# A three-tile input load cut into two around the value weights, and six matmuls on ones behind the first transposes

## The chip, the cores and the metric

The kernel runs on one core of a Trainium2 chip. The metric is the device time of one execution in microseconds (us). The engines are named as in the profile: PE is TensorE's matmuls, PEld its weight loads, DVE VectorE, ACT ScalarE, POOL GpSimd and SP SyncE, which here only issues transfers (DMAs). SPq and PEq are the instruction sequencers of SP and PE.

## What is computed

One block on x of 2048 tokens by 512 channels, bfloat16, with 32 heads of 16 and a hidden width of 1792. Layer norm feeds a linear attention with softmax feature maps and a gated bilinear unit; both are added to x.

```python
xn = _layernorm(x, axis=-1)
q, k, v = xn @ wqkv                      # three parts of 512 columns, 32 heads of 16
pq, pk = q @ w_phi, k @ w_phi            # 16 by 16 for each head
phi_q = concat([softmax(pq), softmax(-pq)])
phi_k = concat([softmax(pk), softmax(-pk)])
kv, z = einsum("bhsf,bhsd->bhfd", phi_k, v), einsum("bhsf->bhf", phi_k)
o = (phi_q @ kv) / (phi_q . z + 1e-6)
h = (xn @ w_gate) * (xn @ w_up)
out = x + o @ wo + h @ w_down
```

## The kernel before

The tokens are 16 tiles of 128. All work is recorded first, as steps: a step belongs to one engine and holds one instruction, or on PE a group of matmuls, with what it reads and writes. From the regions that the steps touch, `_Sched` derives who waits for whom. Then `_order` (L790) writes the order of each engine's queue by list scheduling: it takes the step that can start first by its own cost figures (`cost`, `lat`, and for a transfer `at`, the time at which it is taken to land). Each engine then runs its queue strictly in that order, with semaphore waits where a step needs another engine's result. So an `at` in the source is no time of the chip, but it moves instructions in the queues.

The start of the program is what the change touches.

- SP's queue, in order: x of tile 0 (L352, 128 KB), x of tiles 1 to 3 in one transfer (L353, 384 KB), the two halves of the value weights (L354, 256 KB each: 128-row groups 0 and 1, then 2 and 3), gate and up weights for the first four of 14 column blocks (L357, 512 KB each), w_phi (L358), x of tiles 4 to 7 (L360), the key weights by a transposing transfer (L361), two more pairs of gate and up weights, and behind these the transposing transfers of the normalised tiles 4 and on, each of which waits for DVE.
- PE begins with 30 matmuls of a constant tile of ones (L367) into PSUM bank 3. They compute nothing that is used; they run while the first x is on its way.
- Tiles 0 to 3 (`RAW = 4`, loop at L727) are not normalised before they are used. For each, `emit_centred` (L416) takes the row sum (L424 on DVE, for tile 2 an ACT activation with an accumulator, L420) and makes 512 x minus the sum (L427). `emit_T` (L472) transposes the centred tile on PE by four 128x128 matmuls with an identity, in two halves of two, and ACT copies each half out of PSUM (L277). `emit_moments` (L412, L413 and L414) and `emit_root` (L433: L434 and L437 on POOL) compute the variance and its root, which come in later as a scale. `k_pe` (L552) multiplies the transposed tile by the value weights: four matmuls of 128x512, one for each 128-row group, so the first two need the first half of the value weights and the last two the second. For tiles 0 to 3 these four are separate steps, so the scheduler can put other work between them.
- Then come `make_wbd` (L391, four POOL multiplications, L393), `wprime` (L493), which folds w_phi into the key weights by 32 small matmuls, and the main loop: key softmaxes for all tiles beside the gate and up matmuls (`glu`, L585), the kv sums, the same for the queries, and the output matmuls (`final`, L684).

PE's queue before starts so: 30 matmuls on ones; tile 0's four transposes; tile 0's first value matmul; the transposes of tiles 1 and 2; four value matmuls (tile 0's other three and tile 1's first); tile 3's transposes; the other eleven value matmuls; five groups of four gate and up matmuls; `wprime`. DVE's queue: row sum and centring of tile 0, of tile 1, centring of tile 2, row sum and centring of tile 3, then L386 (a mask) and the moments of tiles 0 to 3.

All matmuls are issued from line 297 and all plain ACT copies from line 277, so groups have to be told apart by shape and time.

Of the kernel before, what the change touches and what calls it, by code (L numbers as in the profile page):

```python
# [12 lines left out]
PE, ACT, DVE, POOL, SP = "PE", "ACT", "DVE", "POOL", "SP"  # L13
# [168 lines left out]
def bass_parallel_sum__linear_kernel_hedgehog__glu_gated_bilinear__prompt_kernel(  # L182
    nc: bass.Bass,
    A_x: bass.AP,
    A_wqkv: bass.AP,
    A_w_phi: bass.AP,
    A_wo: bass.AP,
    B_x: bass.AP,
    B_w_gate: bass.AP,
    B_w_up: bass.AP,  # L190
    B_w_down: bass.AP,
    out: bass.AP,
):
    with ExitStack() as es:
        _build(nc, es, A_x, A_wqkv, A_w_phi, A_wo, B_w_gate, B_w_up, B_w_down, out)


def _build(nc, es, A_x, A_wqkv, A_w_phi, A_wo, B_w_gate, B_w_up, B_w_down, out):
# [59 lines left out]
    def sbv(name, lo, n):  # L258
        off = layout[name] + lo
        return arena[:, off:off + n]  # L260
# [5 lines left out]
    def bank(b, lo=0, n=512):  # L266
        return psum[:, b * 512 + lo: b * 512 + lo + n]

    sc = _Sched(nc)
# [16 lines left out]
    def dve(fn, reads, writes, n, rate=1.0, fixed=65.0, prio=None):  # L286
        return sc.step(DVE, fn, reads=reads, writes=writes, cost=fixed + rate * n / 0.96, lat=150.0, prio=prio)
# [4 lines left out]
    def mms(items, prio=None, cold=False):  # L292

        def fn(e):
            ins = None
            for o, l, r, a, z in items:
                ins = e.matmul(o, lhsT=l, rhs=r, start=a, stop=z)  # L297
            return ins
        reads = []
        writes = []  # L300
        c = 0.0
        for o, l, r, a, z in items:
            reads += [l, r]
            writes.append(o)
            c += max(25.0, o.free_size() / 2.4 + 2.3) * (1.92 if cold else 1.0)
        return sc.step(PE, fn, reads=reads, writes=writes, cost=c, lat=260.0, prio=prio)
# [12 lines left out]
    def x_tile(t):  # L319
        return sbv("x", t * 512, 512)  # L320
# [7 lines left out]
    wv_v = sbv("wv", 0, NQ * 512).rearrange("p (q j) -> p q j", q=NQ)  # L328
# [7 lines left out]
    def load_x(on, t0, n, at):  # L336
        return sc.dma(on, sbv("x", t0 * 512, n * 512).rearrange("p (t d) -> p t d", t=n),
                      x_flat[t0 * 128:(t0 + n) * 128, :].rearrange("(t p) d -> p t d", p=128), at=at)

    def load_w(on, dst, src, at, issue=500.0):  # L340
        return sc.dma(on, dst, src, at=at, issue=issue)
# [5 lines left out]
    def load_gu(on, f0, n, at):  # L347
        return [load_w(on, v[:, :, f0 * 128:(f0 + n) * 128],
                       src[:, f0 * 128:(f0 + n) * 128].rearrange("(q p) f -> p q f", p=128), at)
                for v, src in ((wg_v, B_w_gate), (wu_v, B_w_up))]  # L350

    load_x(SP, 0, 1, 2950.0)  # L352
    load_x(SP, 1, 3, 4200.0)  # L353
    wv_loads = [load_w(on, wv_v[:, 2 * h:2 * h + 2, :],  # L354
                       A_wqkv[h * 256:(h + 1) * 256, 1024:1536].rearrange("(q p) j -> p q j", p=128), at)
                for on, h, at in ((SP, 0, 5000.0), (SP, 1, 6000.0))]
    load_gu(SP, 0, 4, 8300.0)  # L357
    sc.dma(SP, wphi_v, bass.AP(tensor=A_w_phi.tensor, offset=A_w_phi.offset, ap=[[16, 128], [2048, NQ], [1, 16]]),  # L358
           at=10900.0)
    load_x(SP, 4, 4, 11850.0)  # L360
# [5 lines left out]
    one = nc.const_aps.tensor(1.0, [128, 128], BF16)  # L366
# [45 lines left out]
    def emit_moments(t):  # L412
        dve(lambda e: e.bn_stats(stats_v[:, t, 0:6], x_tile(t)), [x_tile(t)], [stats_v[:, t, 0:6]], 512)  # L413
        dve(lambda e: e.bn_aggr(mv_v[:, t, :], stats_v[:, t, 0:6]), [stats_v[:, t, 0:6]], [mv_v[:, t, :]], 6)  # L414

    def emit_centred(t):  # L416

        total = lnt_v[:, 1, 8 + t:9 + t]
        if t in ACT_MEAN:
            sc.step(ACT, lambda e: e.activation(out=xn_tile(t), in_=x_tile(t), func=ACTF.Copy, accum_out=total),  # L420
                    reads=[x_tile(t)], writes=[xn_tile(t), total], cost=700.0, lat=180.0)
            again = [xn_tile(t)]
        else:
            dve(lambda e: e.tensor_reduce(out=total, in_=x_tile(t), axis=AX.X, op=ALU.add), [x_tile(t)], [total], 512,  # L424
                fixed=130.0)
            again = []
        dve(lambda e: e.tensor_scalar(out=xn_tile(t), in0=x_tile(t), scalar1=float(D), scalar2=total, op0=ALU.mult,  # L427
                                      op1=ALU.subtract), again + [x_tile(t), total], [xn_tile(t)], 512, rate=0.5)
# [4 lines left out]
    def emit_root(t):  # L433
        pool(lambda e: e.tensor_scalar(out=veps(t), in0=mv_v[:, t, 1:2], scalar1=1e-5, scalar2=float(D * D),  # L434
                                       op0=ALU.add, op1=ALU.mult),
             [mv_v[:, t, :]], [veps(t)], 1)
        pool(lambda e: e.tensor_tensor(out=rstd_v[:, t, 0:1], in0=veps(t), in1=mhalf[:, 0:1], op=ALU.pow),  # L437
             [veps(t), mhalf], [rstd_v[:, t, 0:1]], 1, rate=155.0, fixed=400.0)
# [33 lines left out]
    def emit_T(t):  # L472
        for h in range(2):
            b = (5, 6, 7, 4)[(2 * t + h) % 4]
            mms([(bank(b, q * 128, 128), xn_tile(t)[:, (2 * h + q) * 128:(2 * h + q + 1) * 128], ident, True, True)
                 for q in range(2)], cold=t < 2)
            act_op(xnT_v[:, 2 * h:2 * h + 2, t * 128:(t + 1) * 128],
                   bank(b, 0, 256).rearrange("p (q s) -> p q s", q=2))
# [73 lines left out]
    def k_pe(t):  # L552
        b = next_a()
        items = group(bank(b), [(xnT(q, t * 128, 128), wv_v[:, q, :]) for q in range(NQ)])
        if t < RAW:
            for item in items:
                mms([item])
        else:
            mms(items)
        act_op(vext_all[:, t, :, 0:64], bank(b).rearrange("p (c j) -> p c j", c=8), scale=scale_of(t))  # L560
# [166 lines left out]
    for t in range(RAW):  # L727
        first = len(sc.steps)
        emit_centred(t)
        emit_T(t)  # L730
        for st in sc.steps[first:]:
            st.urgent = True
        emit_moments(t)
        emit_root(t)
        k_pe(t)
# [192 lines left out]
```

## Time and profile before

| | us |
|---|---|
| median of 3 runs (lowest to highest) | 221.11 (221.06 to 221.14) |
| the profiled execution's own time | 219.36 |
| its span, first to last instruction | 218.1 |
| PE busy in the span | 213.1 (98%) |
| DVE busy | 194.2 (89%) |
| ACT busy | 116.0 (53%) |
| POOL busy | 10.0 (5%) |
| HBM read / written | 8.67 MB / 2.10 MB |

Matmuls are pipelined, so a busy PE in the profile says only that some matmul is on its way; the spacing of their starts tells whether PE was held up. A few matmul records are missing from the trace, at a regular distance: where the spacing is just one matmul too long, it is a record that is missing. The mean granted clock stands as 1.00 in the profile's tables, for this core without an event behind it, so the clock at the start has to be read from the spacing of equal matmuls.

### The profile page before, as it was taken

The page shows a single profiled execution, that of the slowest core. Times are in us where ns is not written, and L with a number is a line of the kernel's source. Part 1 is how long each engine was busy: PE and PEld are TensorE (multiplying, and loading weights), DVE is VectorE, ACT ScalarE, POOL GpSimd, SP SyncE. Part 2 cuts the span into 40 slices and gives each one's busy share as a digit, 9 for nine tenths or more (in the row PEclk, how much of TensorE's full clock was granted, in tenths as well). Part 3 has the DMA queues.
Part 4 walks back from the last instruction along what each step waited for, and adds up shares of the span by engine and source line. Part 5 has one row for each costly group of instructions (what it writes and reads, how often), then busy time and mean ns, then how long its engine had stood idle before and what let it go on. Part 6 is the DMA issues. An engine that isn't in the chain of part 4 may idle for free.

```text
span 218.1 us, 3598 instructions
## 1 busy us (share of the span) xinstructions
PE 213.1 (98%) x1289; PEld 104.5 (48%) x1312; DVE 194.2 (89%) x551; ACT 116.0 (53%) x195; POOL 10.0 (5%) x29
## 2 busy tenths in 40 slices
PE   7999999999999999999999999999999999999996
PEld 6444444444445544444445444444544444454454
DVE  4787999999999389999998899999999999999532
ACT  4578986548353599965553687553544353121000
POOL 2451000110002000000000000000000000000000
DMA  5999440035901340000000002263466547546931
GB/s 186 321 281 298 113 157 3 0 64 155 310 3 23 75 99 0 0 0 3 0 0 2 3 0 48 52 96 74 96 120 125 109 108 108 125 109 127 141 72 50
DMA packets 47442, 19.91 MB, mean 91 GB/s; under 512 B 37440, under 2 KB 47424, under 8 KB 47424
## 3 DMA queue, kind: packets, MB, share of 16 engines
q1 hardware_dynamic: 47424, 19.69, 39.5%
q8 instruction: 10, 0.16, 0.3%
q14 instruction: 8, 0.07, 0.1%
HBM read 8.67 MB, written 2.10 MB: 49 GB/s over the span
## 4 chain that ended last, share of the span: by engine, by line
PE 77%; DVE 15%; ACT 3%; DMA 2%; issue 2%; SPq 1%; DVEq 0%
PE ps L297 77%; DVE arena L598 4%; DVE arena L542 4%; ACT arena L277 3%; DMA arena<-in_A_wqkv_dram 2%; DVE arena L522 2%; DVE arena L574 2%; DVE arena L571 1%; DVE arena L528 1%; DVE arena L450 1%; DVE arena L481 1%; SPq L165 1%; DVE arena L703 0%; DVE arena L452 0%; DVEq L887 0%
## 5 line engine op out<-in xcount | busy, mean ns | idle before, releaser
L297 PE MATMUL ps<-arena 128*128 128x512 bf16 (+5 forms) x1259 | 209.9, 327 | 2.3 <-ACT arena L277 1.0
L297 PEld LDWEIGHTS ps<-arena 128*128 128x128 bf16 (+1 forms) x1282 | 101.4, 98 | 110.8 <-ACT arena L277 1.7
L277 ACT ACTIVATE arena<-ps 128x512 bf16<-128x512 f32 (+2 forms) x140 | 72.0, 571 | 45.5 <-PE ps L297 38.5
L277 ACT ACTIVATE arena<-arena 128x1024 bf16<-128x1024 bf16 (+1 forms) x40 | 38.5, 977 | 30.0 <-DVE arena L528 29.8
L542 DVE TENSOR_TENSOR arena<-arena 128x512 f32<-128x512 bf16 (+3 forms) x128 | 48.5, 389 | 0.2
L598 DVE TENSOR_TENSOR arena<-ps,arena 128x512 bf16<-128x512 f32 x56 | 38.1, 681 | 3.5 <-PE ps L297 2.3
L522 DVE TENSOR_TENSOR arena<-arena 128x64 bf16<-128x64 bf16 (+3 forms) x128 | 31.2, 269 | 3.8 <-ACT arena L277 3.6
L528 DVE TENSOR_TENSOR arena<-arena 128x1024 bf16<-128x1024 bf16 x32 | 21.6, 677 | 0.1
L703 DVE TENSOR_TENSOR arena<-ps,arena 128x512 bf16<-128x512 f32 (+2 forms) x13 | 8.3, 641 | 7.1 <-PE ps L297 7.1
L574 DVE TENSOR_TENSOR arena<-arena 128x1024 bf16<-128x1024 bf16 x16 | 10.8, 676 | 0.0
L277 ACT ACTIVATE arena<-ps,arena 128x512 bf16<-128x512 f32 x12 | 7.9, 682 | 2.8 <-PE ps L297 1.7
L571 DVE RECIPROCAL arena<-arena 128x64 bf16<-128x64 f32 x16 | 8.7, 541 | 0.0
L675 DVE TENSOR_TENSOR arena<-ps,arena 128x512 bf16<-128x512 f32 x12 | 8.1, 676 | 0.1
L450 DVE BATCH_NORM_STATS2 arena<-arena 128x6 f32<-128x512 bf16 x12 | 8.0, 680 | 0.0
L667 DVE RECIPROCAL arena<-ps 128x32 f32<-128x32 f32 x16 | 5.5, 346 | 1.8 <-PE ps L297 1.8
L654 DVE TENSOR_TENSOR arena<-arena 128x512 bf16<-128x512 bf16 x16 | 6.6, 411 | 0.0
L651 DVE RECIPROCAL arena<-arena 128x32 f32<-128x32 f32 x16 | 5.4, 336 | 0.0
L481 DVE TENSOR_SCALAR arena<-arena 128x512 bf16<-128x512 bf16 x12 | 4.3, 399 | 0.7 <-POOL arena L458 0.7
L424 DVE TENSOR_REDUCE arena<-arena 128x1 f32<-128x512 bf16 x3 | 2.0, 683 | 3.1 <-DMA arena<-in_A_x_dram 3.1
L297 PE MATMUL ps<-const-bfloat16-1.0 128*128 128x128 bf16 x30 | 3.4, 313 | 0.8 <-PEq L913 0.8
L297 PEld LDWEIGHTS ps<-const-bfloat16-1.0 128*128 128x128 bf16 x30 | 3.1, 149 | 0.8 <-issue 0.8
L458 POOL TENSOR_TENSOR arena<-arena 128x4 f32<-128x4 f32 x3 | 3.1, 1047 | 0.3
(31 smaller groups left out, 29.7 us busy)
## 6 DMA issues: line engine op xcount, KB each, us to landing
out_dram<-arena SPq DMA_DIRECT2D x15, 128.0 KB, 2.0
arena<-in_B_w_down_dram SPq DMA_DIRECT2D x1, 1792.0 KB, 7.5
arena<-in_B_w_gate_dram SPq DMA_DIRECT2D x2, 640.0 KB, 6.8
arena<-in_B_w_up_dram SPq DMA_DIRECT2D x2, 640.0 KB, 8.0
arena<-in_A_x_dram SPq DMA_DIRECT2D x1, 1024.0 KB, 5.8
arena<-arena SPq DMA_TRANSPOSE x44, 2.6
arena<-in_A_wqkv_dram SPq DMA_DIRECT2D x2, 256.0 KB, 4.0
arena<-in_B_w_gate_dram SPq DMA_DIRECT2D x1, 512.0 KB, 5.3
```

The lines of the kernel that those rows point to most:

```text
L277: return e.activation(out=out_ap, in_=in_ap, func=func, scale=scale, **kw)
L297: ins = e.matmul(o, lhsT=l, rhs=r, start=a, stop=z)
L450: dve(lambda e, t=t: e.bn_stats(stats_v[:, t, 0:6], x_tile(t)), [x_tile(t)], [stats_v[:, t, 0:6]], 512)
L522: dve(lambda e, dst=dst, src=src, k=k: e.tensor_tensor(out=dst, in0=src[:, :, 0:k], in1=src[:, :, k:2 * k], op=ALU.max), [src], [dst], 16 ...
L528: dve(lambda e: e.tensor_tensor(out=p4, in0=p4, in1=src[:, :, None, :].to_broadcast([128, 16, 16, 4]), op=ALU.subtract), [pst, src], [pst] ...
L542: dve(lambda e, dst=dst, src=src, k=k: e.tensor_tensor(out=dst, in0=src[:, :, 0:k], in1=src[:, :, k:2 * k], op=ALU.add), [src[:, :, 0:2 * ...
L571: dve(lambda e: e.reciprocal(out=rs, in_=sm), [sm], [rs], 64, rate=6.0)
L574: dve(lambda e: e.tensor_tensor(out=e4, in0=e4, in1=r4[:, :, None, :].to_broadcast([128, 16, 16, 4]), op=ALU.mult), [ek_v[:, t, :], rs], [ ...
L598: dve(lambda e: e.tensor_tensor(out=dst, in0=bank(bu), in1=gr, op=ALU.mult), [bank(bu), gr], [dst], 512, prio=-1.0)
L654: dve(lambda e: e.tensor_tensor(out=e1, in0=e1, in1=rs[:, :, None, :].to_broadcast([128, 8, 16, 4]), op=ALU.mult), [e1, rs], [e1], 512, ra ...
L675: dve(lambda e: e.tensor_tensor(out=o4, in0=n4, in1=w4, op=ALU.mult), [nd[:, :, 0:64], w], [o], 512)
L703: dve(lambda e: e.tensor_tensor(out=og, in0=ob, in1=xs, op=ALU.add), [ob, xs], [og], c1 - c0, prio=-2.0)
```

## The change

The load of x for tiles 1 to 3 is cut in two: tiles 1 and 2 (256 KB) stay ahead of the value weights' halves, tile 3 (128 KB) goes behind them. The due times (`at`) of these and of the first gate and up weights are set anew. Behind tile 0's transposes, six more matmuls on the constant ones are put on PE, into bank 3 as the 30 at the start, made dependent on the transposes so that they stand behind them.

```diff
     load_x(SP, 0, 1, 2950.0)
-    load_x(SP, 1, 3, 4200.0)
-    wv_loads = [load_w(on, wv_v[:, 2 * h:2 * h + 2, :],
-                       A_wqkv[h * 256:(h + 1) * 256, 1024:1536].rearrange("(q p) j -> p q j", p=128), at)
-                for on, h, at in ((SP, 0, 5000.0), (SP, 1, 6000.0))]
-    load_gu(SP, 0, 4, 8300.0)
+    def load_v(h, at):
+        return load_w(SP, wv_v[:, 2 * h:2 * h + 2, :],
+                      A_wqkv[h * 256:(h + 1) * 256, 1024:1536].rearrange("(q p) j -> p q j", p=128), at)
+
+    load_x(SP, 1, 2, 3850.0)
+    load_v(0, 5050.0)
+    load_v(1, 6200.0)
+    load_x(SP, 3, 1, 6500.0)
+    load_gu(SP, 0, 4, 8600.0)
...
         emit_T(t)
         for st in sc.steps[first:]:
             st.urgent = True
+        if t == 0:
+            mms([(bank(3, 0, 128), one, one, True, True)] * 6, cold=True).deps.append(sc.by_eng[PE][-2])
         emit_moments(t)
```

What the scheduler makes of it: on PE the six matmuls on ones stand between tile 0's transposes and its first value matmul, and tile 3's transposes move behind nine value matmuls where they stood behind five. On DVE, L386 and tile 0's moments instruction (L413) move ahead of tile 3's row sum, and tile 1's aggregation (L414) moves behind tile 2's L413. SP has one transfer more, the fifth of its queue. Behind that, PE's queue holds the same instructions in the same order.

## The prediction

> **What bounds the kernel now.** I read the page first, then the chain of waits, then the timeline of the first 16 us, then what PE waited for and the windows of the span.
>
> ```profile
> PE 213.1 (98%) x1289; PEld 104.5 (48%) x1312; DVE 194.2 (89%) x551; ACT 116.0 (53%) x195; POOL 10.0 (5%) x29
> PE 77%; DVE 15%; ACT 3%; DMA 2%; issue 2%; SPq 1%; DVEq 0%
> ```
>
> PE ends the run, but its busy time hides stalls, so I go to the chain (start, length, what):
>
> ```profile
> 2.23 4.33 DMA arena<-in_A_wqkv_dram
> 6.57 0.05 issue
> 6.61 1.04 PE ps L297 x7
> 7.71 6.65 PE ps L297 x30
> ...
> 95.82 10.74 PE ps L297 x49
> 106.56 0.05 issue
> 106.61 10.74 PE ps L297 x49
> ```
>
> 49 records start 10.79 us (106.61 - 95.82) before the next group. With one missing record that is 50 matmuls of 0.216 each: 512 columns with no gap. So from 6.6 on PE runs dense, and before it the chain is one transfer: the second half of the value weights (issued 2.23, landed 6.57). Now the first 16 us:
>
> ```profile
> 0.83 3.36 PE L297 MATMUL ps<-const-bfloat16-1.0 128*128 128x128 bf16 x30 [0.83 <-PEq L913]
> 2.94 0.69 DVE L424 TENSOR_REDUCE arena<-arena 128x1 f32<-128x512 bf16 x1 [2.94 <-DMA arena<-in_A_x_dram]
> ...
> 4.07 0.61 PE L297 MATMUL ps<-arena 128*128 128x128 bf16 x4
> 4.21 0.63 ACT L420 ACTIVATE arena<-arena 128x512 bf16<-128x512 bf16 x1 [2.15 <-DMA arena<-in_A_x_dram]
> 4.21 0.69 DVE L424 TENSOR_REDUCE arena<-arena 128x1 f32<-128x512 bf16 x1 [0.20 <-DMA arena<-in_A_x_dram]
> ...
> 5.52 9.40 PE L297 MATMUL ps<-arena 128*128 128x512 bf16 x79 [0.84 <-ACT arena L277]
> ...
> 6.18 0.35 DVE L427 TENSOR_SCALAR arena<-arena 128x512 bf16<-128x512 bf16 x1
> ...
> 6.61 7.24 PEld L297 LDWEIGHTS ps<-arena 128*128 128x128 bf16 x38 [0.39 <-DMA arena<-in_A_wqkv_dram]
> ...
> 11.69 1.83 POOL L393 TENSOR_TENSOR arena<-arena 128x128 bf16<-128x128 bf16 x4
> ```
>
> PE alone between 6.4 and 6.8 us:
>
> ```profile
> 6.18 0.83 PE L297 MATMUL ps<-arena 128*128 128x512 bf16 x2
> ```
>
> There are two stalls. Tile 0's last transpose starts at 4.36 (4.07 + 0.61, less a length of 0.31); PE issues nothing more until 5.52. The row names ACT, but ACT had made the first copy by 5.2 (L277, from 4.84, 0.38 for one), and the first half of the value weights landed at 5.38 (issued 1.71, 3.7 to landing): that is what released PE. The second stall is the weight load at 6.61, 0.05 after the second half landed. The last views tell how far a gain at the start reaches:
>
> ```profile
> PE ps L297 <- ACT arena L277: 1.0, 2, 0.8
> PEld ps L297 <- DMA arena<-in_A_wqkv_dram: 0.4, 1, 0.4
> ```
>
> ```profile
> 15.08:23.20 8.12, 8.12 (x38) 3.72 (x38) 6.36 (x21) 7.09 (x14) 1.27 (x2) 1.00 1.21 280
> 23.20:58.30 35.10, 34.89 (x161) 15.87 (x163) 35.08 (x92) 23.60 (x39) 1.37 (x2) 1.00 0.38 110
> 58.30:218.10 159.80, 156.97 (x980) 76.74 (x996) 143.00 (x416) 76.54 (x126) 1.26 (x2) 1.00 0.32 62
> ```
>
> These waits are nearly all that PE has (columns of the windows: length, then busy PE, PEld, DVE, ACT, POOL, clock, DMA share, GB/s). PE's work after 6.6 is the same in both kernels, so whatever it starts earlier there it should end earlier.
>
> **The transfers.** x of tile 0 lands at 2.9 (0.79 + 2.1) in both. The three-tile load lands at 4.2 (1.25 + 2.9), 0.43 per tile. The weight halves follow at 5.38 and 6.57, 1.19 each. So tiles 1 and 2 land near 2.9 + 2 x 0.43 = 3.77, and the halves one tile earlier, by 0.43: at 4.95 and **6.14**. Bounds for the second half: tile 3's bytes cost 0.59 at the halves' own rate (5.98), or 0.35 at the best rate shown, 376 GB/s between 6 and 7 us (6.22). Tile 3's x now closes the same megabyte that the second half closed: **6.57**. Bounds: 6.45, if the new order spares the slow stretch between 4 and 5 us (242 GB/s against 336 before it) some 0.1; above, if it finishes in step with the next 128 KB of the gate load, which takes (8.06 - 6.57)/4 = 0.37: 6.94.
>
> **PE, step by step.** The ones of the start come every 0.105 ((3.36 - 0.31)/29, 0.31 being one matmul's own length). Six cost 0.64 at that pace, from 4.47 to 5.11, and lie wholly in the first stall. The first value matmul needs the first half (4.95 + 0.10, the distance seen before: 5.05) and ACT's copy. ACT's copy stood behind L420, which with its accumulator held ACT from 4.21 to 4.84; now L420 starts at 3.8, and the copy waits only for tile 0's transposes: 4.50 + 0.36 = 4.86. So the ones decide: 5.11, **0.40 earlier** than 5.52. Were the clock full by then, six would take 0.33 and 5.05 would decide; the cost of the ones is 0 to 0.06, and I take 0.06 (a gain of their own is the clock rival, below). The transposes of tiles 1 and 2 take (6.18 - 5.52 - 0.216)/8 = 0.055 each, 5.52 being tile 0's first value matmul and 6.18 its second; with two value matmuls PE is at 5.99. DVE is in time: tile 1 centred by 4.01 + 0.69 + 0.35 = 5.05, tile 2 by 5.35, needed at 5.33 and 5.55.
>
> Next late is the second half: 6.14 + 0.05 = 6.19 against 6.61, 0.42 earlier. Seven more value matmuls at 0.216 bring PE to 7.70, at tile 3's transposes. Next late is their input: landing 6.57, L424 0.69, L427 0.35 and 0.11 of hand-overs: **7.72**. DVE would have waited for x from 5.99 on; L386 and one L413 fill the time before that. From there PE has 4 x 0.055 + 27 x 0.216 = 6.05 to `wprime`: 13.77. Before, tile 3's transposes started three matmuls after 6.61, at 7.27, and the count runs 7.27 + 0.22 + 31 x 0.216 = 14.19. **Gain 0.42.** The two gates are about level, so either being late shows in full and either being early gains nothing: I take 0.40.
>
> **What must be ready 0.4 earlier.** POOL: tile 3's sum and centring now hold DVE at 6.59 to 7.66, and tile 1's aggregation ends near 9.08 (8.73 before). POOL's second root then ends 0.09 later, and the four L393, which follow without a break, end at 13.61 for 13.52. PE needs them at 13.77: 0.16 of cover; beyond it, every 0.1 costs 0.1. The added issue takes SP 0.47 to 0.51 (rows of its neighbours), and everything behind it on SP is issued that much later. In full, that means: gate 8.06 to 8.6, needed 9.45; up 9.75 to 10.25, needed 10.32; w_phi 9.9 to 10.4, needed 11.7; x of tiles 4 to 7 11.3 to 11.8, needed 12.4; key weights 13.16 to 13.66, needed 13.77. All are covered, up and key weights by 0.1 only. I take no delay: these transfers land 5 to 8 us after their issue, so they queue for bytes, and the bytes are the same. The later gate and up loads land over 1 us before use, and the transposing transfers wait on DVE.
>
> **The sum.** 218.1 - 0.40 = 217.7 of span; 219.36 - 0.40 = 218.96 for that execution. The median stands 1.75 above the profiled execution; I carry the difference over: 221.11 - 0.40 = **220.7**. What a measurement of this kernel can tell from no change is 0.2%, 0.44 us, so the forecast stands just inside it.
>
> **Rivals.** *Tile 3 late* (the other side). The end moves by (landing of tile 3's x) - 6.99, since landing + 1.15 + 6.05 is to be held against 14.19. In step with the gate load's first quarter (6.94) the gain is 0.05. At 6.99 it is gone, at 7.43 the run is 0.2% slower, and landing together with the whole gate load (8.06) costs 1.07: 222.2. For it: five loads are under way at once, and a load has landed only with its last piece. Against it: before, loads landed in the order of their issue, at steps that fit their bytes.
>
> [...]
>
> *Given back to DVE.* From 23.2 to 58.3 DVE is busy 35.08 of 35.10 us and the chain runs through it. If its sequence does not move, PE arrives early and waits: gain 0 to 0.2, 220.9 to 221.1. Against: ahead of it DVE has 1.76 idle in 8.12 us, waiting for what PE and ACT make, and behind it idles 16.8 of 159.8; so it should move along.
>
> *The clock.* The ones may do more than fill. Equal matmuls come every 0.105 until 4.4 and every 0.055 at 5.8, so the clock doubled in or just after the stall. If timed executions, which take 1.75 longer than the profiled one, stay at half pace longer because PE falls idle at 4.5, the ones keep it busy and win some of that: up to 1.75, 219.4. Against: the profiled execution was at full pace in spite of the idle time, and three timed runs agree within 0.08. [...]
>
> **How the numbers follow.** Forecast (gain 0.2 to 0.65) 0.62; tile 3 late 0.16; given back 0.13; clock 0.09. Faster by over 0.2%: 0.47 of the forecast's share (both gates a little early) and the clock case, 0.38. Slower by over 0.2%: two thirds of tile 3 late, and a little for the thin covers, 0.12. The rest, 0.50, lies within. The range takes in the early bounds with part of the clock case (220.1) and tile 3 landing at 7.4 (221.5).
>
> **What would show it.** Right: first value matmul at 5.1, the second half's wait ended near 6.2, tile 3's transposes at 7.7, `wprime` near 13.9, the last PE group ending 0.4 earlier. Wrong: a DMA wait above 0.3 before tile 3's L424 beyond 6.6; PE waits on POOL or a transfer before `wprime`; new PE waits on DVE between 17 and 58; matmuls still 0.105 apart after 5.2.

## The result

| | before | after |
|---|---|---|
| median of 22 runs (lowest to highest), us | 221.09 (219.19 to 223.09) | 219.74 (219.10 to 220.20) |
| runs above 220.7 | 14 of 22 | 0 of 22 |
| the profiled execution's own time | 219.36 | 219.10 |
| its span | 218.1 | 217.8 |

The ratio after to before is 0.9959, with a 95% interval of 0.9940 to 0.9977: faster by 0.2 to 0.6%, or 0.9 us (0.0041 x 221.09). The medians differ by more, 1.35, since the median of before lies in the upper of two groups of runs. The forecast was 220.7, a gain of 0.40. The median of 219.74 lies below the range's lower end of 220.1; by the ratio it would be 220.2 (221.11 x 0.9959), just inside. The profiled pair differs by 0.26 only.

The runs of before fall into two groups with a gap between 220.18 and 220.96: eight around 219.8 and fourteen around 221.2. The three runs shown at the start (221.06 to 221.14) all came from the upper group, and the profiled execution from the lower one. These 22 runs of the changed kernel have no upper group.

### The profile page after: what moved, and what is told of

It is laid out like the page before. It is cut to its first block, busy times and chain, and to the rows that moved or that the text cites. A ratio compares the mean times of both kernels' runs of the same rounds, so it can differ in the third digit from the quotient of the medians.

```text
span 217.8 us, 3610 instructions
## 1 busy us (share of the span) xinstructions
PE 213.0 (98%) x1295; PEld 104.5 (48%) x1318; DVE 194.2 (89%) x551; ACT 116.0 (53%) x195; POOL 10.0 (5%) x29
## 4 chain that ended last, share of the span: by engine, by line
PE 77%; DVE 15%; ACT 3%; issue 2%; DMA 2%; SPq 1%; DVEq 0%
PE ps L297 77%; DVE arena L602 4%; DVE arena L546 4%; ACT arena L277 3%; DMA arena<-in_A_wqkv_dram 2%; DVE arena L526 2%; DVE arena L578 2%; DVE arena L575 1%; DVE arena L532 1%; DVE arena L454 1%; DVE arena L485 1%; SPq L165 1%; DVE arena L707 0%; DVE arena L456 0%; DVEq L893 0%
## 5 line engine op out<-in xcount | busy, mean ns | idle before, releaser
L428 DVE TENSOR_REDUCE arena<-arena 128x1 f32<-128x512 bf16 x3 | 2.1, 684 | 3.5 <-DMA arena<-in_A_x_dram 3.5
```

## The profile after

The page of the changed kernel, its busy time, its chain and its groups:

```profile
PE 213.0 (98%) x1295; PEld 104.5 (48%) x1318; DVE 194.2 (89%) x551; ACT 116.0 (53%) x195; POOL 10.0 (5%) x29
...
PE 77%; DVE 15%; ACT 3%; issue 2%; DMA 2%; SPq 1%; DVEq 0%
...
L297 PE MATMUL ps<-const-bfloat16-1.0 128*128 128x128 bf16 x36 | 3.6, 282 | 0.8 <-PEq L919 0.8
```

The ones are x36 for x30; apart from them no engine's busy time moved by more than 0.1 us (PE 213.1, ACT 116.0 before). The timeline of the changed kernel's first 16 us (start, length, engine; lines from L354 on now stand four lower in the source, so L424 of before is L428, L393 is L397):

```profile
0.83 3.09 PE L297 MATMUL ps<-const-bfloat16-1.0 128*128 128x128 bf16 x30 [0.83 <-PEq L919]
...
4.14 0.40 PE L297 MATMUL ps<-arena 128*128 128x128 bf16 x4 [0.23 <-DVE arena L431]
...
4.38 0.51 PE L297 MATMUL ps<-const-bfloat16-1.0 128*128 128x128 bf16 x6
...
4.90 0.88 PE L297 MATMUL ps<-arena 128*128 128x512 bf16 x9
...
6.33 8.31 PE L297 MATMUL ps<-arena 128*128 128x512 bf16 x70 [0.55 <-DMA arena<-in_A_wqkv_dram]
6.66 0.69 DVE L428 TENSOR_REDUCE arena<-arena 128x1 f32<-128x512 bf16 x1 [0.54 <-DMA arena<-in_A_x_dram]
...
7.79 0.60 PEld L297 LDWEIGHTS ps<-arena 128*128 128x128 bf16 x7 [0.27 <-DVE arena L431]
...
10.42 3.15 PEld L297 LDWEIGHTS ps<-arena 128*128 128x128 bf16 x16 [0.30 <-DMA arena<-in_B_w_up_dram]
...
11.84 1.83 POOL L397 TENSOR_TENSOR arena<-arena 128x128 bf16<-128x128 bf16 x4
...
13.99 1.98 PEld L297 LDWEIGHTS ps<-arena 64*128 64x128 bf16 x40 [0.42 <-DMA arena<-in_A_wqkv_dram]
```

The long gap from 4.68 to 5.52 is closed: tile 0's transposes, six ones, first value matmul at 4.90. The wait for the second half of the value weights is still there and ends at 6.33 (6.61 before). Tile 3's transposes start behind a DVE wait near 7.8, and `wprime` (the 64-row weight loads) at 13.99, 14.28 before. At 10.42 there is a wait that before did not have: for the up weights. In all 14 traces of this study, 201.78 or 201.79 us lie between `wprime`'s first weight load and the start of PE's last matmul. So the differences between these kernels, and between two executions of one, arise ahead of `wprime`, in the first 14 to 17 us; only e12's end is 0.6 us later on top of that (2.45 us behind PE's last matmul, 1.84 or 1.85 elsewhere).

The weight load of `wprime` in the kernel before:

```profile
14.28 1.77 PEld L297 LDWEIGHTS ps<-arena 64*128 64x128 bf16 x39 [0.42 <-issue]
```

## The experiments

Theory A, the forecast: the new order of the loads brings the second half and all behind it forward; the ones only fill. Theory B, the clock: with PE idle behind tile 0's transposes, part of the executions stay at half pace for longer, and the ones prevent it.

One table of the traces first, in us; the text below refers to it. "Full pace" is between the start of the last matmul that is spaced as at half pace (0.107 for 128 columns, 0.427 for 512) and the first at full pace (0.055, 0.216). "Idle" is PE's idle time between tile 0's transposes, with the ones where they stand behind them, and the next work of the tiles, by the brackets of PE's rows (where another place is named, the idle time there). The four landings are the completions of the loads. "On record" is the time from which the trace records full granted clock; eight of the traces hold such a record, and the views of the profile do not print it.

| trace | full pace | on record | idle | second half | gate | up | key weights | `wprime` |
|---|---|---|---|---|---|---|---|---|
| before | 4.36 to 5.52 | - | 0.84 | 6.57 | 8.06 | 9.75 | 13.16 | 14.28 |
| e3 before again | 8.68 to 9.08 | 8.93 | 0.68 | 6.66 | 8.35 | 10.15 | 13.51 | 15.64 |
| e2 ones only | 3.66 to 3.85 | 3.82 | 0.46 | 6.63 | 8.30 | 10.01 | 13.41 | 14.34 |
| e9 ones only | 4.87 to 5.39 | - | 0.18 | 6.86 | 8.31 | 10.02 | 13.40 | 14.57 |
| e8 halves due later | 6.00 to 6.22 | - | 0.22 | 6.59 | 8.20 | 10.01 | 13.38 | 14.46 |
| after | 3.34 to 3.52 | 3.46 | under 0.2 | 6.29 | 8.69 | 10.38 | 13.71 | 13.99 |
| e4 after again | 4.81 to 5.00 | 4.95 | 0.19 | 6.87 | 8.68 | 10.35 | 13.66 | 14.58 |
| e10 after again | 6.29 to 6.67 | - | none | 6.15 | 8.18 | 10.30 | 13.62 | 14.32 |
| e1 loads only | 5.64 to 5.84 | - | 0.54 | 6.85 | 9.89 | 11.40 | 14.70 | 15.00 |
| e5 twelve at the start | 6.37 to 7.04 | - | 1.78, ahead of the transposes | 6.48 | 9.75 | 11.25 | 14.56 | 14.85 |
| e6 twelve behind | 5.03 to 5.21 | 5.15 | none | 6.51 | 10.08 | 11.55 | 14.85 | 15.16 |
| e7 x all ahead | 4.30 to 4.51 | 4.49 | 1.85 | 7.37 | 9.61 | 11.05 | 14.39 | 15.34 |
| e11 one value load | 3.87 to 4.12 | 4.09 | 0.32 | 5.89 | 7.76 | 9.45 | 12.88 | 14.04 |
| e12 three loads | 9.58 to 10.32 | 10.19 | 0.93, ahead of the transposes | 6.46 | 8.28 | 9.98 | 13.32 | 16.67 |

**The loads alone.** The changed kernel without the six ones behind tile 0.

```diff
-        if t == 0:
-            mms([(bank(3, 0, 128), one, one, True, True)] * 6, cold=True).deps.append(sc.by_eng[PE][-2])
```

> The new load order without the six matmuls on ones. Transfer theory (the earlier value weights make the whole gain of 1.35 us in the median): median as the changed kernel, 219.7 +- 0.3, with its narrow spread of about 1 us. Clock theory (some executions stay at half pace for some 3.4 us more when PE idles behind tile 0's transposes, which costs up to 1.7 us; the ones prevent it, and the loads alone are worth about 0.3): median 220.3 to 220.9, spread over 2 us, since the idle time is still about 0.5 us long.

219.90 (219.06 to 221.57, 12 runs), before 220.40 beside it, ratio 0.9976 [0.9946, 1.0007]; 2 of 12 runs above 220.7, against 14 of 29 of before. The median fits theory A (219.7 +- 0.3) and misses what theory B expected (220.3 to 220.9); the interval of the ratio holds 1, so the run decides little by itself. PE's weight loads in its trace:

```profile
5.12 0.14 PEld L297 LDWEIGHTS ps<-arena 128*128 128x128 bf16 x2 [0.77 <-ACT arena L277]
...
8.35 0.61 PEld L297 LDWEIGHTS ps<-arena 128*128 128x128 bf16 x7 [0.26 <-DVE arena L431]
...
11.44 3.13 PEld L297 LDWEIGHTS ps<-arena 128*128 128x128 bf16 x16 [0.75 <-DMA arena<-in_B_w_up_dram]
15.00 0.90 PEld L297 LDWEIGHTS ps<-arena 64*128 64x128 bf16 x35 [0.42 <-DMA arena<-in_A_wqkv_dram]
```

The wait for the up weights, 0.30 in the changed kernel's profile, is 0.75 here. From the weight load of tile 3's transposes to `wprime` PE takes 6.20 when nothing else is late (13.99 - 7.79; the second trace of the changed kernel has 14.58 - 8.37 = 6.21). Here it takes 6.65, so the late up weights cost 0.45.

**The ones alone.** The kernel before with the same two lines put in, its loads untouched.

> The old load order with the six matmuls on ones. Transfer theory: as the kernel before, 221.1 +- 0.2 in the median, spread over 2 us. Clock theory: median 219.9 to 220.3 and a spread of about 1 us, as of the changed kernel, but some 0.3 later because the second half of the value weights still lands near 6.6.

219.91 (219.02 to 220.60, 12 runs), ratio 0.9968 [0.9940, 0.9996]; none above 220.7. Theory B expected 219.9 to 220.3, theory A 221.1. So the ones alone take the upper group away. Either part alone ends at the same median here: the parts do not seem to add, though for the loads alone the gain is not clear of noise.

**Before again**, unchanged (no edit), as a run of its own.

> The kernel before once more, for a second trace of it and more times. Clock theory: times in two groups, near 219.8 and near 221.3; if this trace is one of the slow group, its matmuls are 0.107 us (128 columns) and 0.427 us (512 columns) apart for up to 3.4 us after 5.5. Transfer theory: every trace has full pace from 5.5 on, and a slow execution shows later landings instead.

220.52 (219.16 to 223.37, 12 runs), ratio 0.9987 [0.9949, 1.0024]; 5 of 12 above 220.7. This profile caught an execution above the split (220.74). PE's first value matmul and then its weight loads in it:

```profile
5.39 10.89 PE L297 MATMUL ps<-arena 128*128 128x512 bf16 x79 [0.68 <-ACT arena L277]
```

```profile
5.39 0.19 PEld L297 LDWEIGHTS ps<-arena 128*128 128x128 bf16 x2 [0.94 <-ACT arena L277]
...
7.08 0.15 PEld L297 LDWEIGHTS ps<-arena 128*128 128x128 bf16 x1 [0.28 <-issue]
7.50 0.15 PEld L297 LDWEIGHTS ps<-arena 128*128 128x128 bf16 x1 [0.28 <-ACT arena L277]
7.93 0.15 PEld L297 LDWEIGHTS ps<-arena 128*128 128x128 bf16 x1 [0.28 <-issue]
8.36 6.86 PEld L297 LDWEIGHTS ps<-arena 128*128 128x128 bf16 x34 [0.28 <-issue]
15.64 0.43 PEld L297 LDWEIGHTS ps<-arena 64*128 64x128 bf16 x26 [0.42 <-issue]
```

One weight load goes with each value matmul. From 7.08 to 8.36 they come every 0.42 or 0.43, half the pace of 0.216; the profile names a wait (ACT) for one of them only, and its step is no longer than the others. In the first trace of this kernel `wprime` came at 14.28; here it comes 1.36 later, and the span is 219.5 for 218.1. The delay of this execution is PE's clock, which the trace records as full only from 8.93 on.

**After again**, the changed kernel without an edit.

> The changed kernel once more, for a second trace and more times. [...]

219.93 (219.11 to 221.70, 12 runs), before 221.11, ratio 0.9964 [0.9937, 0.9990]; one run above 220.7, at 221.70, so with the six ones too an execution can come out that late. It was not profiled.

**Fewer ones at the start**, with the changed kernel: PE idles ahead of tile 0's transposes in place of behind them.

```diff
-    mms([(bank(3, 0, 128), one, one, True, True)] * 30, cold=True)
+    mms([(bank(3, 0, 128), one, one, True, True)] * 12, cold=True)
```

> The changed kernel with 12 instead of 30 matmuls on ones at the start, so that PE idles from about 2.1 to 4.1 us. [...] Transfer theory: the ones hide behind the first load anyway, 219.7 +- 0.2.

220.47 (219.58 to 221.10, 12 runs), ratio 0.9988 [0.9962, 1.0015]; 4 of 12 above 220.7. Nothing that is used was taken away and the first x lands as before, yet the median is 0.54 above the changed kernel's beside it, and 4 of 12 runs are above 220.7 for 1 of 12. Resampling the runs gives -0.1 to 1.1 for the difference of medians, so an idle PE seems to cost time even where nothing waits for PE, but this run alone does not show it. The profiled execution was one of the faster ones (219.94); its clock doubled between 6.37 and 7.04.

**Twelve ones behind tile 0** in place of six, with the planner's cost for them halved so that the order stays.

```diff
-            mms([(bank(3, 0, 128), one, one, True, True)] * 6, cold=True).deps.append(sc.by_eng[PE][-2])
+            filler = mms([(bank(3, 0, 128), one, one, True, True)] * 12, cold=True)
+            filler.deps.append(sc.by_eng[PE][-2])
+            filler.cost /= 2
```

> The changed kernel with 12 instead of 6 ones behind tile 0's transposes, all else in the same order. Clock theory: nothing left to win, since six already close the gap; in executions whose doubling is early the 12 end near 5.05 and cost nothing, in late ones they end near 5.7 and cost up to 0.6: median 219.8 to 220.1, highest up to 220.9. If more activity brings the doubling forward (a count of matmuls decides): 219.4 or less.

219.91 (219.26 to 220.46, 12 runs), ratio 0.9964 [0.9937, 0.9992]; none above 220.7. With the idle time filled, six more ones brought nothing here (219.93 with six, in the run of the changed kernel above).

**x of tile 3 in a load of its own, but ahead of the halves**, with the six ones.

```diff
-    load_x(SP, 1, 3, 4200.0)
+    load_x(SP, 1, 2, 4200.0)
+    load_x(SP, 3, 1, 4200.0)
```

> The old order of bytes (x of tiles 1 and 2, x of tile 3, then the two halves) with the six ones, so that only the extra transfer is new beside the run with ones alone. If transfers only queue for bytes: gate, up and key weights land as in the old order (8.1 to 8.4, 9.8 to 10.2, 13.2 to 13.5), times as with ones alone, 219.9 +- 0.2. If the extra issue delays all that is behind it on SP: they land 0.4 to 0.6 later (8.7, 10.4, 13.9), as in the trace of the changed kernel, and the median is up to 0.3 higher.

220.18 (219.77 to 222.91, 12 runs), ratio 0.9987 [0.9949, 1.0024]; 4 of 12 at 221.8 or above. The first half landed at 6.67 (4.67 to 5.38 elsewhere), and gate, up and key weights at 9.61, 11.05 and 14.39, later than either expectation. PE in this trace:

```profile
4.40 0.56 PE L297 MATMUL ps<-const-bfloat16-1.0 128*128 128x128 bf16 x6
6.81 9.50 PE L297 MATMUL ps<-arena 128*128 128x512 bf16 x81 [1.85 <-DMA arena<-in_A_wqkv_dram]
```

PE was idle for 1.85 us, but the clock had doubled by 4.51, and it stayed up: the matmuls from 6.81 on are 0.055 and 0.216 apart. In this execution an idle time of this length behind the doubling did no harm. That it never does is not shown. Two of the four late runs (221.87 and 222.91) list a mean granted clock of 0.992, a loss that 3.5 us at half pace would make (0.008 x 220.6 / 0.5). The half pace ahead of the first recorded step does not count in that mean: e3 lists 1.00 with its clock full only from 8.93 on. So in these two the clock seems to have fallen back. The other two list 1.00 and fit executions that were still at half pace when the idle time began. None of the four was profiled.

**The second half's due time raised** in the kernel with the old loads and the six ones, so that PE's queue puts tile 1's first two value matmuls and tile 3's transposes ahead of the wait.

```diff
-                for on, h, at in ((SP, 0, 5000.0), (SP, 1, 6000.0))]
+                for on, h, at in ((SP, 0, 5000.0), (SP, 1, 7000.0))]
```

> The loads of before with the six ones; only the planner's due time of the second value half is raised from 6000 to 7000, which puts tile 1's two first-half value matmuls and tile 3's transposes ahead of the wait for the second half. Theory (only the first 14 us count, the second half's landing is a gate, PE stalls ahead of it): PE fills 0.4 to 0.6 us of its idle time, wprime starts near 13.9 (14.34 with the six ones alone), and the median falls by 0.3 to 0.5 below the six ones alone: 219.3 to 219.7. Rival (something before wprime, the up weights or POOL, decides instead): no difference, 219.9, with a new PE wait on the up weights or on POOL between 10 and 14 us.

219.52 (219.10 to 219.75, 12 runs), ratio 0.9942 [0.9907, 0.9976]: 0.19 below the ones alone and with the narrowest spread of all. The wait for the second half is gone from PE, but in this trace the clock doubled only at 6.2, so `wprime` came at 14.46, not near 13.9. The gain was in the direction expected, at about half its size.

**The ones alone and the changed kernel on the same chip**, for the worth of the loads (no further edit in either).

> The loads of before with the six ones, as in e2_ones_only, here on the same chip as the changed kernel. If the new order of the loads is worth its 0.4 us, this is 0.3 to 0.4 slower than the changed kernel; if the added transfer gives it back by landing the up and key weights later, the two agree within 0.2.

> The changed kernel once more, as the partner of the other runs. Expected 219.6 to 219.9, with its up weights landing after 10.3 as in every trace with the added transfer.

219.71 (219.29 to 221.03) and 219.70 (219.05 to 220.47), 12 runs each: no difference, so in the median the new order of the loads brought nothing that can be told. Resampling gives -0.5 to 0.5, so a worth of the loads of 0.3 is not excluded. The second trace also shows what the ones do not do: with PE never waiting between 4 and 16 us, the clock still doubled only after 6.29, and `wprime` came at 14.32.

**All value weights in one transfer** of 512 KB in the changed kernel: four transfers ahead of the gate weights, as before, with the changed kernel's bytes.

```diff
...
-    load_v(0, 5050.0)
-    load_v(1, 6200.0)
+    load_w(SP, wv_v, A_wqkv[:, 1024:1536].rearrange("(q p) j -> p q j", p=128), 6200.0)
```

> The changed kernel with both halves of the value weights in one transfer of 512 KB, so that four transfers stand ahead of the gate weights as before, with the same bytes. If the number of transfers ahead is what delays the gate and up weights, they land as before (gate 8.0 to 8.4, up 9.7 to 10.2, key weights 13.1 to 13.5); if it is their order or the 128 KB transfer behind the weights, they land late as in the changed kernel (up 10.35 to 11.5, key 13.7 or later). PE's first value matmul has to wait for all value weights, near 6.3, so the time itself should be 0.5 to 1.0 above the changed kernel: 220.3 to 220.9.

219.28 (219.03 to 220.38, 10 runs), ratio 0.9953 [0.9916, 0.9989], and a miss in the time: 0.42 below the changed kernel's median beside it, where 0.5 to 1.0 above was expected. PE in its trace:

```profile
5.11 0.66 PE L297 MATMUL ps<-arena 128*128 128x128 bf16 x8 [0.32 <-DVE arena L426]
5.94 10.36 PE L297 MATMUL ps<-arena 128*128 128x512 bf16 x79 [0.17 <-DMA arena<-in_A_wqkv_dram]
```

All 512 KB landed at 5.89, before the second half did in any other trace (6.15 at the earliest), and PE waited 0.17. Gate, up and key weights landed earlier than in any other trace, and earlier than either expectation. The wait for the up weights is gone.

**Three transfers ahead of the gate weights:** x of tiles 1 to 3 in one load as before, the value weights in one load, the six ones (the edit is shown against the kernel before).

```diff
-    wv_loads = [load_w(on, wv_v[:, 2 * h:2 * h + 2, :],
...
-                for on, h, at in ((SP, 0, 5000.0), (SP, 1, 6000.0))]
+    load_w(SP, wv_v, A_wqkv[:, 1024:1536].rearrange("(q p) j -> p q j", p=128), 6000.0)
```

> x of tiles 1 to 3 in one transfer as before, then all value weights in one transfer of 512 KB, with the six ones: three transfers ahead of the gate weights (before: four, the changed kernel: five), the same bytes. If each transfer ahead costs the later ones about 0.3 us beside its bytes, everything lands as early as with the one value load behind tiles 1 and 2 or earlier: value weights by 6.2, gate by 7.8, up by 9.5, key weights by 13.0, wprime near 13.8 to 14.1 and the median 219.0 to 219.4. If the early landings of that run were chance, the value weights land near 6.6 as the second half did before, PE waits for them that long, wprime comes near 14.4 and the median is 219.7 to 220.

219.97 (219.74 to 222.40, 13 runs), ratio 0.9969 [0.9940, 0.9998]; 3 of 13 above 220.7. The median fits the second expectation. The profiled execution was the slowest of the 13 (222.40). Its PE:

```profile
3.66 0.53 PE L297 MATMUL ps<-const-bfloat16-1.0 128*128 128x128 bf16 x3
5.11 0.61 PE L297 MATMUL ps<-arena 128*128 128x128 bf16 x4 [0.93 <-DVE arena L425]
5.51 0.85 PE L297 MATMUL ps<-const-bfloat16-1.0 128*128 128x128 bf16 x6
6.19 10.11 PE L297 MATMUL ps<-arena 128*128 128x128 bf16 x46
```

Here x of tile 0 landed at 3.96 instead of 2.8 to 3.0, PE was idle for 0.93 ahead of tile 0's transposes, where no ones stand, and the clock was full only from 10.19 on. It is e3's delay by the clock again, behind another idle time. That each transfer ahead costs a fixed time is not borne out: with one fewer than in the run before, nothing landed earlier. But this trace has that late first load in it, so what sets the early landings of the run before stays open.

## Why the prediction was right or wrong

Its steps against the profiled execution (us):

| step | forecast | measured |
|---|---|---|
| x of tiles 1 and 2 | 3.77 | 3.83 |
| first half | 4.95 | 4.67 |
| second half (bounds 5.98 to 6.22) | 6.14 | 6.29 |
| x of tile 3 (bounds 6.45 to 6.94) | 6.57 | 6.64 |
| first value matmul | 5.11 | 4.90 |
| second half's wait ended | 6.19 | 6.33 |
| tile 3's transposes | 7.72 | 7.85 |
| the four POOL multiplications end | 13.61 | 13.67 |
| `wprime` | 13.77, "near 13.9" | 13.99 |
| the end earlier by | 0.40 | 0.28 |

**The mechanism of the forecast fits this pair.** The gates were the ones named, and the gain passed undiminished to the end. The start of PE's last group, from the chains of the kernel before and of the changed one:

```profile
207.65 8.64 PE ps L297 x57
```

```profile
207.37 8.64 PE ps L297 x57
```

0.28 earlier, as `wprime` was by 0.29. "Given back to DVE" did not happen. The size of the second half's step was off: it landed 0.28 earlier, not 0.43, though the first half landed 0.71 earlier. How much of the 0.28 the new order made cannot be told from one pair: the second half of the changed kernel landed at 6.15, 6.29 and 6.87 in its three traces. The first value matmul came at 4.90 since in this execution the clock was already up: six ones took 0.33, not 0.64, and ACT's copy decided.

**The step that failed for the median** is "The median stands 1.75 above the profiled execution; I carry the difference over", with the argument against the clock rival that "three timed runs agree within 0.08". The difference was not constant: it was the upper group, which the change all but removes. Of all 150 runs of before, e3's among them, 85 lie above 220.7, around 221.33, and the other 65 around 219.77; with more runs the gap between the groups fills in (220.65 to 220.97). The changed kernel's 46 runs have one above 220.7 and a median of 219.81; the ones alone, 24 runs, one and 219.83. So the new kernel is as fast as the lower group of the old one, not faster; what it wins is that the upper group is all but gone. The clock rival, given 0.09, named the mechanism, and its 219.4 was 0.3 too low. That the median moved the way of the forecast was therefore in good part luck: the path that it followed made 0.28 at most in the profiled pair, not the 1.35.

**What the traces show of the clock.** On record the full clock lasts 215.04 us in six traces and 211.63 in e3 and e12. These differ by 3.41, and 215.04 is 63 times 3.413, 211.63 is 62 times: by an estimate from these two lengths, the clock's changes in these traces lie whole multiples of 3.41 us apart. In the eleven traces without a long idle time ahead of the doubling (all but e3, e5 and e12; before's 0.84 lies within its bracket of 4.36 to 5.52) the clock doubled at times spread from 3.3 to 6.7 us.

In e3 (idle 0.68 behind the transposes) and e12 (0.93 ahead of them) it doubled at 8.93 and 10.19, 2.26 and 3.52 us behind the latest time that the eleven allow (6.67). In e1, with 0.54 behind the transposes, it had doubled by 5.84. That fits ones that work by filling the idle time: with them alone, 1 of 24 runs lies above 220.7. That the earlier first half works by shortening it, which would be why each part alone does nearly the whole, is argued from e1's 0.54 and not shown.

The length of an idle time does not settle the matter. In the changed kernel's own trace PE had no matmul until 0.83, which is longer than e3's 0.68, and the clock was full from 3.46 on. How much idle time delays the doubling, and where it has to lie, is not shown: only two traces have such a late doubling, and in e5, with 1.78 idle ahead of the transposes, the clock doubled between 6.37 and 7.04.

The granted clock that is listed with the single runs points to a second kind of delay. Of 128 runs of before that list it, 21, all at 221.51 or above, have 0.992, as the two of e7; none of the changed kernel's 46 and none of the 24 with the ones alone has. In these the clock seems to have fallen back for some 3.5 us. None was profiled, so what made it do so stays open.

**The step that failed in the traces** is "I take no delay: these transfers ... queue for bytes, and the bytes are the same". With the added transfer ahead of them the loads landed about as late as the prediction's own figures "in full", or later: gate 8.6, up 10.25, key weights 13.66 there, 8.69, 10.38 and 13.71 in the profile, and up between 10.30 and 11.55 in the seven traces with five transfers ahead, against 9.45 to 10.15 in the seven with three or four. Only e10's gate and key weights were a little earlier (8.18, 13.62). The profile's 0.30 wait for the up weights cost nothing beyond the count, but 0.45 in e1 and, by the same reckoning, 15.16 - 8.01 - 6.20 = 0.95 in e6, where PE waited for the gate weights too. What the second half wins by its earlier place (6.15 to 6.87, on average 6.53, against 6.57 to 6.86, on average 6.66, in the five traces with the old loads in two halves) is 0.14 where the prediction had 0.43. So it is small beside these delays, which fits a gain of 0.28 in the profiled pair and none that can be told in the median. The "tile 3 late" rival did not come: x of tile 3 landed 0.34 to 0.41 behind the second half in all six traces that have it there, which is about what its own 128 KB take (0.35 at the prediction's 376 GB/s).

**A faster version?** One value load (219.28) and the later due time (219.52) have lower medians than the changed kernel beside them (219.70). Resampling the runs puts the one at -0.42 with a 95% interval of -0.91 to 0.26 for the difference of medians, the other at -0.19 (-0.73 to 0.21). Neither is shown to be faster than the changed kernel. Their combination was not tried.

## What to carry to other kernels

A median that stands far above the profiled execution is a finding, not an offset: look at all the runs for a second group before carrying it over, since a change may remove the group without touching the path that the profile shows. Look at idle time on PE ahead of the doubling of its clock, even where PE waits for something else anyway: in e3, 0.68 us of it went with half pace up to 8.93 and a span longer by 1.4 us (219.5 for 218.1). Here six cheap matmuls in the gap, the loads as they were, went with 1 of 24 runs above 220.7, for 85 of 150 without them; in the changed kernel twelve brought no more than six (219.91 for 219.93). A transfer put into a queue ahead of others went with later landings behind it although the bytes stayed the same (up weights at 10.30 to 11.55 for 9.45 to 10.15): cost the loads behind it at their later issue in full.

## What the runs showed of the hardware

- In two executions of the same kernel, both with less than 1 us of idle time on PE behind the first transposes, `wprime` came at 14.28 and at 15.64: in the first the clock had doubled by 5.52, in the second at 8.93.
- The full clock on record lasted 215.04 us in six traces and 211.63 in two, 63 and 62 times 3.413: steps of 3.41 us, by an estimate from these two lengths. In eleven traces it doubled between 3.3 and 6.7 us, in e3 and e12 at 8.93 and 10.19.
- Once the clock had doubled, 1.85 us of idle time did not bring the half pace back in one trace (x all ahead); two other runs of that kernel list a granted clock of 0.992.
- One transfer of 512 KB landed whole at 5.89 (one trace); the same bytes in two transfers landed at 6.15 to 6.87, in the same place of the queue.
- The landings of one kernel vary between executions by more than the change was meant to move them: the second half at 6.29, 6.87 and 6.15 in three traces of the changed kernel.
